# Narrowing 64-bit weights in an attention and MLP kernel: a parametric ReLU in place of a scaled copy and an and-or

## The chip, the cores and the metric

One core of a Trainium2 chip runs the whole program. It has TensorE for matrix products and transposes, VectorE and ScalarE for work along rows, GpSimd, SyncE that issues the transfers here, and 16 DMA engines. The metric is the device time of one execution in microseconds (us), lower is better.

## What is computed

The reference is an attention followed by two MLPs. The weights of both MLPs reach the kernel as 64-bit floats and are read as pairs of 32-bit words.

```python
# attention: q, k rotated; batch 4, 8 heads, 576 positions, 64 wide
scores = (1 / sqrt(64)) * (q_rot @ k_rot.T)
attn = exp(scores - max(scores)); attn = attn / (sum(attn) + 1e-09)
x = attn @ v                      # as 2304 tokens x 512
# first MLP: 512 -> 1536 -> 512
xn = x / sqrt(mean(x * x) + 1e-06) * rms_g
g = xn @ w_gate
x = (g * sigmoid(g) * (xn @ w_val)) @ w_out
# second MLP: 512 -> 1024 -> 1024 -> 512
h = ((x @ w1) * (x @ w2)) @ w3
out = h @ w_out
```

## The kernel before

Attention takes the heads in 16 pairs. A pair has nine tiles of 128 rows of scores. For each tile TensorE makes the scores (tile s), VectorE the row maximum (nm), ScalarE the Exp (p), TensorE the transposes (tp), ScalarE the high half and VectorE the low half of the transposed probabilities (pt), and TensorE the product with v (pv, two stages of it per pair). All matrix products are split into a high half, which is a cast to the fast float type, and a low half, which is what the cast left over; three products of halves (PASS) make one.

The first MLP works in six chunks of 384 tokens. Its input is scaled by the row norm (xr, function zz, line 684), transposed on TensorE (xp), and split (xc). For each of 12 slices of the hidden width TensorE makes gate and value (mm, line 308, 24 matmuls a slice), ScalarE the Silu (sg), VectorE the gated product u, ScalarE and VectorE the two halves of u (us), and TensorE the product with the output weights (acc, line 828, 12 matmuls a slice). The second MLP follows; most of its weights are narrowed while the first runs.

A weight is narrowed in steps. Its raw words (wraw, one buffer of 512 KB for 128x512 numbers) are loaded by SyncE. Step n0 is a scaled copy on ScalarE in place: the high word, read as a float, times 2^-111, which moves the exponent to that of a 32-bit float. Step n1 on VectorE shifts the low word right by 29 places; n2 shifts the high word left by 3 and puts the low word's bits in (the or, to tile wt). As the shift drops the sign, n3 takes the sign bit out of the high word and puts it into wt (the and-or). Then n4 on ScalarE casts the high half and n5 subtracts for the low half. These steps are a unit: 36 units for the first MLP, three for each of 12 slices (gate, value, output weights). For the second MLP function conv does the first four steps, 40 times, in jobs between the slices.

The order of work is fixed in two ways. Inside the attention it is written out by hand: ORDER gives the place of each step in a pair, ONCE that of each step of the first six units (W0.0 to W5.5, where W3.5 is step n3 of unit 5), and the first MLP's preparation. From unit 6 on, the units are written after the attention's program, and a scheduler places each instruction on its engine by its own estimate of when inputs and buffers are free. It can place them into the attention, as it does with the loads of units 6, 7 and 10 and the first steps of unit 10. Raw buffers come from a pool of three and, from the last pair on, from a second pool of two; a load must wait until the last reader of its buffer is done. PSUM tiles of transposes and matmuls come from one pool of four banks.

Of the kernel before, what the change touches and what calls it, by code (L numbers as in the profile page):

```python
# [8 lines left out]
F32 = mybir.dt.float32  # L9
F32R = mybir.dt.float32r  # L10
U32 = mybir.dt.uint32
I32 = mybir.dt.int32
AF = mybir.ActivationFunctionType
ALU = mybir.AluOpType
# [16 lines left out]

ONCE = {"WF.0": 0.058, "WF.1": 0.481, "W0.0": 2.871, "W1.0": 3.803, "W2.0": 4.815, "W0.1": 7.205, "W3.0": 7.711,
# [8 lines left out]
WARM = (22, 18, 3, 26)  # L41
NORM_AT = {5: (0, 1), 6: (1, 4), 7: (4, 6), 8: (6, 9), 9: (9, 12), 10: (12, 15), 11: (15, 18)}
# [21 lines left out]
def f(ap):  # L64
    return ap.bitcast(F32)
# [3 lines left out]
def kernel(  # L69
# [21 lines left out]
    nc = tc.nc  # L91
# [23 lines left out]
    def words(a):  # L115
        return a.bitcast(U32)
# [52 lines left out]
    wt_p = rpool("wt", WT)  # L169
# [37 lines left out]
    def rows(w, i, h=0):  # L207
        return words(w)[i * 128:(i + 1) * 128, h * 1024:(h + 1) * 1024]

    def unit(load, done):  # L210

        u = {}

        def raw():
            if not u:
                a = fifo.pop(0)
                u["lo"], u["hi"] = a[..., 0], a[..., 1]

        def n0():
            raw()
            nc.scalar.activation(out=f(u["hi"]), in_=f(u["hi"]), func=AF.Copy, scale=2.0**-111)

        def n1():
            raw()
            nc.vector.tensor_scalar(out=u["lo"], in0=u["lo"], scalar1=29, scalar2=None, op0=ALU.logical_shift_right)

        def n2():
            u["t"] = wt_p.tile([128, 512], F32, tag="t", name="wt")  # L230
            nc.vector.scalar_tensor_tensor(out=u["t"].bitcast(U32), in0=u["hi"], scalar=3, in1=u["lo"],
                                           op0=ALU.logical_shift_left, op1=ALU.bitwise_or)

        def n3():
            t = u["t"].bitcast(U32)
            nc.vector.scalar_tensor_tensor(out=t, in0=u["hi"], scalar=0x80000000, in1=t, op0=ALU.bitwise_and, op1=ALU.bitwise_or)

        return load, [n0, n1, n2, n3] + done(u)

    lo_eng = [nc.gpsimd]  # L240

# [9 lines left out]
    def unit_gv(kind, i, s):  # L251
        w = (w_gate, w_val)[s]

        def get():
            if s == 0:
                wgv[kind, i] = wtile([128, 2, 2, 512], "wgv", "wgv", i)
            return wgv[kind, i][:, 0, s], wgv[kind, i][:, 1, s]
        return unit(lambda: fetch(cols(w, i), 1), lambda u: split_steps(u, get))

    def unit_wo(kind, i):  # L260
        def get():
            t = wo[kind, i] = wtile([128, 2, 512], "wo", "wo", i)
            return t[:, 0], t[:, 1]
        return unit(lambda: fetch(rows(w_out, i)), lambda u: split_steps(u, get))
# [494 lines left out]
    def at(t, fn, *a):  # L759
        ev.setdefault(int(t // 1), []).append((t, len(ev.get(int(t // 1), ())), fn, a))  # L760
# [12 lines left out]
    once = {"NX": xload, "rst": rst, "nwt": nwt}  # L773
    for n_, t in ONCE.items():
        n_, u = n_.split(".") if "." in n_ else (n_, 0)
        u = int(u)
        if n_ == "WF":
            at(t, prefetch, u + 1)
        elif n_[0] == "W":
            at(t, units[u][1][int(n_[1])])  # L780
            if n_ == "W5":
                st[1] = max(st[1], u + 1)
        elif n_ in once:
            at(t, once[n_], 0)
        else:
            at(t, dict(sq=sq, z=zz, xp=xp, xh=xh, xl=xl)[n_[:-1]], 0, int(n_[-1]))
# [55 lines left out]
    def conv(src, c=None):  # L842

        u = {}

        def load():
            u["raw"] = raw = wst.tile([128, 512, 2], U32, tag="raw", name="wraw")
            if c is None:
                nc.sync.dma_start(out=raw.rearrange("p n t -> p (n t)"), in_=src)
            else:  # L850
                nc.sync.dma_start(out=raw.rearrange("p (c n) t -> p c (n t)", c=KC), in_=src.rearrange("(c p) n -> p c n", p=128))

        def rest():
            raw = u["raw"]
            lo, hi = raw[..., 0], raw[..., 1]
            nc.scalar.activation(out=f(hi), in_=f(hi), func=AF.Copy, scale=2.0**-111)
            nc.vector.tensor_scalar(out=lo, in0=lo, scalar1=29, scalar2=None, op0=ALU.logical_shift_right)
            t_ = wt_p.tile([128, 512], F32, tag="t", name="wt")
            t = t_.bitcast(U32)
            nc.vector.scalar_tensor_tensor(out=t, in0=hi, scalar=3, in1=lo, op0=ALU.logical_shift_left, op1=ALU.bitwise_or)  # L860
            nc.vector.scalar_tensor_tensor(out=t, in0=hi, scalar=0x80000000, in1=t, op0=ALU.bitwise_and, op1=ALU.bitwise_or)
            return t_
        return load, rest

    def tt(o, x, y, op=ALU.subtract):
# [156 lines left out]
    def gtile(shape, dt=F32):  # L1022
        return gv.tile(shape, dt, tag="g", name="gv")
# [82 lines left out]
    for k, batch in enumerate(todo):  # L1106
        run = []
        for g, s, P in batch:
            if (g, s) not in ws:
                ws[g, s] = weights(g, s)  # L1110
            t = gtile([128, 4, CH])
# [19 lines left out]
        n_ = (g + 1, s) if P == 2 else None  # L1131
# [60 lines left out]
    for i in range(NCH):  # L1192
# [9 lines left out]
        for o in range(NR):  # L1202
            t = gtile([128, DM])
# [62 lines left out]
```

## Time and profile before

| | |
|---|---|
| runs | 1107.41, 1105.12 and 1101.75 us, median 1105.12 |
| profiled execution | span 1101.9 us, granted TensorE clock 0.995 of full speed on average |
| busy share | TensorE 98%, VectorE 62%, ScalarE 51%, GpSimd 22% |
| attention | until about 309 us |
| first MLP | from there until about 770 us |

The span runs from the first to the last instruction of the one execution that was profiled. It is close to the fastest of the three runs and 3.2 us below their median. A row of the timeline below names the start, the duration, the engine, the line of the program, the operation, and what it writes and reads; in brackets stands the idle time of the engine just before it and what ended it.

### The profile page before, as it was taken

To read this page: it belongs to the slowest core of one execution; us is meant where nothing else is said; L and a number is where in the kernel's file an instruction comes from. 1 tells how busy PE (TensorE), PEld (TensorE's weight loads), DVE (VectorE), ACT (ScalarE), POOL (GpSimd) and SP (SyncE) were. 2 spreads that over 40 slices of the span, in tenths; PEclk is the share of its full clock that TensorE was granted. 3 is DMA by queue.
4 is the path that set the end of the run, shared out by engine and by line. 5 is a ranking of instruction groups with operands and counts; after the bars stand their busy time and mean duration, and the time that the engine had idled before them with its cause. 6 is when DMAs were issued, how large, how long until landed. Compare 5 with 4: busy or idle time off the path is not lost.

```text
span 1101.9 us, 18536 instructions
## 1 busy us (share of the span) xinstructions
PE 1077.5 (98%) x6669; PEld 1040.8 (94%) x6669; DVE 680.4 (62%) x1278; ACT 557.0 (51%) x1241; POOL 243.3 (22%) x359
## 2 busy tenths in 40 slices
PE   8899999999999999999999999999999999999998
PEld 7899999999889999999999999999999999888886
DVE  7899999999889953357555567552463443633220
ACT  5799998999865532233332333223353434422220
POOL 6878888799300000000000000000000000000000
PEclk9899999999999999999999999999999999999999
DMA  7677777776356531168492485635931415603441
GB/s 205 159 203 198 204 176 184 201 198 155 78 176 190 173 115 58 43 215 268 145 302 81 170 282 196 225 102 205 355 124 57 139 68 174 227 1 130 128 144 58
DMA packets 123547, 179.33 MB, mean 163 GB/s; under 512 B 18496, under 2 KB 85568, under 8 KB 123456
## 3 DMA queue, kind: packets, MB, share of 16 engines
q1 hardware_dynamic: 123456, 178.15, 53.6%
q8 instruction: 53, 0.87, 0.3%
q14 instruction: 38, 0.31, 0.1%
HBM read 99.53 MB, written 50.07 MB: 136 GB/s over the span
## 4 chain that ended last, share of the span: by engine, by line
PE 72%; DMA 11%; POOL 6%; DVE 5%; issue 2%; SPq 2%; ACT 1%; POOLq 0%; DVEq 0%; ACTq 0%
PE mm L308 22%; PE ps L1057 13%; PE acc L828 11%; PE ps L1200 9%; PE ps L1160 4%; PE s L496 4%; PE pv L569 3%; PE tp L513 3%; POOL rtmp L383 2%; DMA raw<-in_q_dram 2%; POOL rot L377 2%; DMA x2D<-x 1%; DMA vr<-in_v_dram 1%; DMA ks<-xy 1%; DMA xs<-xsD 1%
## 5 line engine op out<-in xcount | busy, mean ns | idle before, releaser
L308 PE MATMUL mm<-xc,wgv 128*128 128x384 f32 x1728 | 316.2, 335 | 0.2 <-ACT wgv L245 0.2
L308 PEld LDWEIGHTS mm<-xc,wgv 128*128 128x128 f32 x1728 | 299.9, 188 | 0.8 <-ACT wgv L245 0.7
L1057 PE MATMUL ps<-xs,cw 128*128 128x384 f32 x1008 | 176.3, 335 | 1.2 <-DMA xs<-xsD 1.2
L1057 PEld LDWEIGHTS ps<-xs,cw 128*128 128x128 f32 x1008 | 174.6, 188 | 2.1 <-DMA xs<-xsD 1.9
L828 PE MATMUL acc<-us,wo 128*128 128x384 f32 x864 | 166.2, 335 | 2.4 <-ACT us L107 2.2
L828 PEld LDWEIGHTS acc<-us,wo 128*128 128x128 f32 x864 | 150.7, 188 | 4.2 <-ACT us L107 3.2
L496 PE MATMUL s<-ks,qs 128*128 128x288 f32 x640 | 122.3, 318 | 8.6 <-DMA ks<-xy 5.0
L501 DVE TENSOR_REDUCE nm<-s 128x1 f32<-128x576 f32 x144 | 107.8, 750 | 14.2 <-PE s L496 12.5
L507 ACT ACTIVATE p<-s,nm 128x576 f32<-128x576 f32 x144 | 107.5, 746 | 10.8 <-DVE nm L501 10.2
L496 PEld LDWEIGHTS s<-ks,qs 128*128 128x128 f32 x640 | 91.8, 193 | 11.5 <-issue 5.5
L1200 PE MATMUL ps<-wp,us 128*128 128x512 f32 x432 | 98.1, 389 | 0.0
L1200 PEld LDWEIGHTS ps<-wp,us 128*128 128x128 f32 x432 | 81.1, 188 | 16.8
L107 ACT CAST us<-u 128x384 fp32r<-128x384 f32 x72 | 36.8, 511 | 119.0 <-DVE u L320 115.0
L521 DVE TENSOR_TENSOR pt<-tp,pt 128x512 fp32r<-128x512 f32 x144 | 94.5, 681 | 1.3 <-ACT pt L517 0.6
L320 DVE SCALAR_TENSOR_TENSOR u<-mm,sg 128x384 f32<-128x384 f32 x72 | 39.8, 553 | 86.1 <-PE mm L308 80.9
L517 ACT CAST pt<-tp 128x512 fp32r<-128x512 f32 x144 | 82.5, 585 | 2.9 <-PE tp L513 2.0
L513 PE MATMUL tp<-idn,p 128*128 128x128 f32 x576 | 83.5, 277 | 0.5 <-DVE x L609 0.2
L569 PE MATMUL pv<-pt,vs 128*128 128x288 f32 x512 | 81.0, 300 | 2.6 <-DVE pt L521 2.5
L569 PEld LDWEIGHTS pv<-pt,vs 128*128 128x128 f32 x512 | 70.8, 188 | 3.1 <-DVE pt L521 3.1
L513 PEld LDWEIGHTS tp<-idn,p 128*128 128x128 f32 x576 | 68.7, 143 | 2.1 <-PE s L496 0.6
L318 ACT ACTIVATE sg<-mm 128x384 f32<-128x384 f32 x72 | 35.1, 488 | 66.1 <-PE mm L308 65.8
L108 DVE TENSOR_TENSOR us<-u,us 128x384 fp32r<-128x384 f32 x72 | 40.0, 556 | 36.3 <-ACT us L107 36.2
(138 smaller groups left out, 1357.0 us busy)
## 6 DMA issues: line engine op xcount, KB each, us to landing
ks<-xy SPq DMA_DIRECT2D x62, 288.0 KB, 5.0
wraw<-in_moe_w_dram SPq DMA_DIRECT2D x32, 512.0 KB, 5.4
xsD<-xo SPq DMA_DIRECT2D x28, 384.0 KB, 3.9
xs<-xsD SPq DMA_DIRECT2D x14, 768.0 KB, 8.2
wraw<-in_moe_w_out_dram SPq DMA_DIRECT2D x20, 512.0 KB, 4.6
qs<-xy SPq DMA_DIRECT2D x62, 160.0 KB, 2.8
uD<-gv SPq DMA_DIRECT2D x12, 768.0 KB, 3.6
us<-uD SPq DMA_DIRECT2D x24, 384.0 KB, 3.9
```

The lines of the kernel that those rows point to most:

```text
L308: nc.tensor.matmul(ps[:, 0:CH], lhsT=w[:, a, s, c * 128:(c + 1) * 128], rhs=x[:, b_, c, :], start=(i == 0), stop=(i == 3 * KC - 1))
L496: nc.tensor.matmul(ps[:, hf, 0:HS], lhsT=l, rhs=r_[:, hf * HS:(hf + 1) * HS], start=(i == 0), stop=(i == n - 1))
L501: nc.vector.tensor_reduce(out=nm, in_=s_ps[p, t][:, :, 0:HS], axis=AX.XY, op=ALU.max, negate=True)
L507: nc.scalar.activation(out=pp.rearrange("p (a b) -> p a b", a=2), in_=s_ps.pop((p, t))[:, :, 0:HS], func=AF.Exp, bias=s_max.pop((p, t)), s ...
L513: nc.tensor.transpose(ps[:, c, :], p_sb[p, t][:, LF + c * 128:LF + (c + 1) * 128], idn)
L517: lastins["act"] = nc.scalar.copy(out=hi, in_=src)
L521: lastins["dve"] = nc.vector.tensor_tensor(out=lo, in0=src, in1=f(hi), op=ALU.subtract)
L569: nc.tensor.matmul(ps[:, 0:HS], lhsT=l.rearrange("p s d -> p (s d)"), rhs=r, start=(i == 0), stop=(i == 8))
L828: nc.tensor.matmul(acc[o][:, 0:CH], lhsT=wo[kind, n][:, a, o * 128:(o + 1) * 128], rhs=us[:, b_], start=(n == first and s == 0), stop=(n = ...
L1057: nc.tensor.matmul(b[ch], lhsT=w[i][:, p_, c * 128:(c + 1) * 128], rhs=x[i][:, r, c], start=(first and ch != 1 and n == 0), stop=(n == 5), ...
L1160: nc.tensor.matmul(p_, lhsT=t[a][:, c], rhs=woc[c][:, b_], start=(i == 0), stop=(i == 3 * NJ - 1))
L1200: nc.tensor.matmul(ac[o], lhsT=us[j // 2][:, a, j % 2, o * 128:(o + 1) * 128], rhs=wp[j][:, b_], start=(j == 0 and s == 0), stop=(j == NJ ...
```

## The change

Step n0 becomes a Prelu: for a positive number the result is the number times 2^-111, as before; for a negative one it is multiplied by 2^32 as well. The larger exponent of the negative numbers sets the bit that n2's shift by 3 moves to the place of the sign. Step n3 is left out, in the units and in conv; in ONCE, n3's entries go, and the two steps behind it are renumbered at the times they had.

```diff
-    "W3.2": 49.378, "sq2": 56.9, "W0.4": 60.614, "W1.3": 61.7, "W5.1": 63.645, "W4.2": 66.556, "W2.3": 69.949,
...
+    "sq2": 56.9, "W0.4": 60.614, "W1.3": 61.7, "W4.1": 63.645, "W3.2": 66.556, "W2.3": 69.949,
...
+    def narrow(hi):
+
+        nc.scalar.activation(out=f(hi), in_=f(hi), func=AF.Prelu, scale=2.0**-111, alpha=2.0**32)
...
         def n0():
             raw()
-            nc.scalar.activation(out=f(u["hi"]), in_=f(u["hi"]), func=AF.Copy, scale=2.0**-111)
+            narrow(u["hi"])
...
-        def n3():
-            t = u["t"].bitcast(U32)
-            nc.vector.scalar_tensor_tensor(out=t, in0=u["hi"], scalar=0x80000000, in1=t, op0=ALU.bitwise_and, op1=ALU.bitwise_or)
-
-        return load, [n0, n1, n2, n3] + done(u)
+        return load, [n0, n1, n2] + done(u)
...
-            if n_ == "W5":
+            if n_ == "W4":
...
         def rest():
             raw = u["raw"]
             lo, hi = raw[..., 0], raw[..., 1]
-            nc.scalar.activation(out=f(hi), in_=f(hi), func=AF.Copy, scale=2.0**-111)
+            narrow(hi)
             nc.vector.tensor_scalar(out=lo, in0=lo, scalar1=29, scalar2=None, op0=ALU.logical_shift_right)
-            t_ = wt_p.tile([128, 512], F32, tag="t", name="wt")
-            t = t_.bitcast(U32)
-            nc.vector.scalar_tensor_tensor(out=t, in0=hi, scalar=3, in1=lo, op0=ALU.logical_shift_left, op1=ALU.bitwise_or)
-            nc.vector.scalar_tensor_tensor(out=t, in0=hi, scalar=0x80000000, in1=t, op0=ALU.bitwise_and, op1=ALU.bitwise_or)
-            return t_
+            t = wt_p.tile([128, 512], F32, tag="t", name="wt")
+            nc.vector.scalar_tensor_tensor(out=words(t), in0=hi, scalar=3, in1=lo, op0=ALU.logical_shift_left, op1=ALU.bitwise_or)
+            return t
```

The scheduler's order moves in more places than the diff names. The first is VectorE's order at the start of the first MLP, behind the second slice's u. Before, these rows stand there (wraw is a shift, wt<-wraw the or, wt<-wraw,wt the and-or, xr the scaling of the second chunk's input, xc its low half):

```order
L320 SCALAR_TENSOR_TENSOR u<-mm,sg 128x384
L675 TENSOR_TENSOR rstd<-rstd,nt 128x3
L231 SCALAR_TENSOR_TENSOR wt<-wraw 128x512
L684 SCALAR_TENSOR_TENSOR xr<-xr,rstd,g 128x512 x3
L227 TENSOR_SCALAR wraw<-wraw 128x512
L108 TENSOR_TENSOR us<-u,us 128x384
L236 SCALAR_TENSOR_TENSOR wt<-wraw,wt 128x512
L699 TENSOR_TENSOR xc<-xp,xc 128x4x128
```

After, an or of unit 8 stands directly ahead of that u, a shift and a norm step directly behind it, and then these rows (line numbers are those of the changed program):

```order
L246 TENSOR_TENSOR wo<-wt,wo 128x512
L671 TENSOR_TENSOR nt<-nt,ms 128x3
L233 SCALAR_TENSOR_TENSOR wt<-wraw 128x512 x3
L106 TENSOR_TENSOR us<-u,us 128x384
L672 TENSOR_TENSOR nt<-cst,nt 128x3
L229 TENSOR_SCALAR wraw<-wraw 128x512
L246 TENSOR_TENSOR wgv<-wt,wgv 128x512 x2
L673 TENSOR_TENSOR rstd<-rstd,nt 128x3
L246 TENSOR_TENSOR wo<-wt,wo 128x512
L229 TENSOR_SCALAR wraw<-wraw 128x512
L233 SCALAR_TENSOR_TENSOR wt<-wraw 128x512 x2
L682 SCALAR_TENSOR_TENSOR xr<-xr,rstd,g 128x512 x3
```

The scaling of xr, which came third behind that u, has moved behind three shifts, four low halves, five ors and us.

The second place is TensorE's order at the same time, from the first matmul of the first MLP. Before:

```order
L308 MATMUL mm<-xc,wgv 128x384 x48
L828 MATMUL acc<-us,wo 128x384 x14
L692 MATMUL xp<-idn,xr 128x128 x4
L308 MATMUL mm<-xc,wgv 128x384 x24
L692 MATMUL xp<-idn,xr 128x128 x4
L828 MATMUL acc<-us,wo 128x384 x10
L692 MATMUL xp<-idn,xr 128x128 x4
```

After:

```order
L306 MATMUL mm<-xc,wgv 128x384 x48
L826 MATMUL acc<-us,wo 128x384 x24
L690 MATMUL xp<-idn,xr 128x128 x4
L306 MATMUL mm<-xc,wgv 128x384 x24
L690 MATMUL xp<-idn,xr 128x128 x8
L306 MATMUL mm<-xc,wgv 128x384 x24
```

All 24 output matmuls of the first two slices now stand ahead of the first transposes of the second chunk's input.

The third place is ScalarE's order in the attention around the narrowing of unit 10. Before, it stands in the last pair (lt is the last tile's part of pt):

```order
L547 CAST lt<-lp 64x512
L507 ACTIVATE p,sums<-s,nm 128x576
L517 CAST pt<-tp 128x4x128
L507 ACTIVATE p,sums<-s,nm 128x576
L517 CAST pt<-tp 128x4x128
L223 ACTIVATE wraw<-wraw 128x512
L517 CAST pt<-tp 128x4x128
```

After, one pair earlier:

```order
L545 CAST lt<-lp 64x512
L505 ACTIVATE p,sums<-s,nm 128x576
L210 ACTIVATE wraw<-wraw 128x512
L515 CAST pt<-tp 128x4x128
L505 ACTIVATE p,sums<-s,nm 128x576
L515 CAST pt<-tp 128x4x128 x2
```

The narrowing now stands ahead of the first cast of its pair instead of the third. Its shift on VectorE and its load on SyncE have moved one pair earlier as well; the load stands right behind that pair's loads of v (vr), as it stood behind the last pair's before. ScalarE's order still has two table loads, at the start and ahead of the first Silu.

## Rows read from the trace of the kernel before

**Rows 1.** Page, part 1: busy us, share of the span, instructions

```profile
PE 1077.5 (98%) x6669; PEld 1040.8 (94%) x6669; DVE 680.4 (62%) x1278; ACT 557.0 (51%) x1241; POOL 243.3 (22%) x359
```

**Rows 2.** Windows of 20 us: length, busy (count) by engine, clock, DMA share, GB/s

```profile
360.00:380.00 20.00, 20.00 (x117) 20.00 (x117) 18.70 (x36) 11.39 (x21) 0.00 (x0) 1.00 0.50 158
...
640.00:660.00 20.00, 20.00 (x117) 20.00 (x116) 12.75 (x25) 8.02 (x16) 0.00 (x0) 1.00 0.87 294
```

**Rows 3.** Groups of VectorE: the and-or; count, busy us, mean ns, idle before

```profile
L861 DVE SCALAR_TENSOR_TENSOR wt<-wraw,wt 128x512 uint32<-128x512 uint32 x40 | 26.7, 686 | 0.4
...
L236 DVE SCALAR_TENSOR_TENSOR wt<-wraw,wt 128x512 uint32<-128x512 uint32 x36 | 25.9, 732 | 0.0
```

**Rows 4.** Groups of ScalarE, columns as in rows 3

```profile
L507 ACT ACTIVATE p<-s,nm 128x576 f32<-128x576 f32 x144 | 107.5, 746 | 10.8 <-DVE nm L501 10.2 <-ACT pt L517 0.2
L517 ACT CAST pt<-tp 128x512 fp32r<-128x512 f32 x144 | 82.5, 585 | 2.9 <-PE tp L513 2.0
...
L223 ACT ACTIVATE wraw<-wraw 128x512 f32<-128x512 f32 x36 | 24.7, 688 | 27.1 <-DMA wraw<-in_moe_w_gate_dram 11.2 <-DMA wraw<-in_moe_w_out_dram 8.2 <-DMA wraw<-in_moe_w_val_dram 7.5
...
L318 ACT ACT_TABLE_LOAD x1 | 1.3, 1283 | 0.0
```

**Rows 5.** Timeline of VectorE and TensorE at two and-ors of the attention

```profile
117.94 0.90 DVE L236 SCALAR_TENSOR_TENSOR wt<-wraw,wt 128x512 uint32<-128x512 uint32 x1
...
121.57 0.77 PE L496 MATMUL s<-ks,qs 128*128 128x288 f32 x4 [0.48 <-ACT p L507]
...
171.80 1.55 DVE L236 SCALAR_TENSOR_TENSOR wt<-wraw,wt 128x512 uint32<-128x512 uint32 x1
...
174.75 0.63 PE L583 MATMUL op<-idn,osb 128*128 128x128 f32 x4 [0.36 <-DVE pt L521]
```

**Rows 6.** Timelines of three engines around the load of unit 10

```profile
278.62 0.68 DVE L236 SCALAR_TENSOR_TENSOR wt<-wraw,wt 128x512 uint32<-128x512 uint32 x1
...
280.34 0.54 SPq L201 DMA_DIRECT2D wraw<-in_moe_w_val_dram  x1
...
284.69 1.15 DVE L227 TENSOR_SCALAR wraw<-wraw 128x512 uint32<-128x512 uint32 x1 [2.10 <-DMA wraw<-in_moe_w_val_dram]
...
286.50 1.34 PE L569 MATMUL pv<-pt,vs 128*128 128x288 f32 x8 [2.55 <-DVE pt L521]
```

**Rows 7.** Windows: length, TensorE's busy time (count), granted clock, DMA share, GB/s

```profile
288.00:291.50 3.50, 3.50 (x17) 0.51 0.00 0
672.00:676.00 4.00, 3.35 (x19) 1.00 0.91 310
```

**Rows 8.** Timelines of three engines one pair earlier

```profile
258.18 0.68 DVE L231 SCALAR_TENSOR_TENSOR wt<-wraw 128x512 uint32<-128x512 uint32 x1
...
262.31 0.61 SPq L348 DMA_DIRECT2D vr<-in_v_dram  x1
...
266.68 1.23 PE L569 MATMUL pv<-pt,vs 128*128 128x288 f32 x8
```

**Rows 9.** Timeline of TensorE at the start of the first MLP

```profile
320.99 0.66 PE L692 MATMUL xp<-idn,xr 128*128 128x128 f32 x4 [0.17 <-DVE xr L684]
...
326.02 1.99 PE L828 MATMUL acc<-us,wo 128*128 128x384 f32 x10
```

**Rows 10.** Timeline of VectorE in the same stretch

```profile
318.63 0.43 DVE L227 TENSOR_SCALAR wraw<-wraw 128x512 uint32<-128x512 uint32 x1 [1.00 <-DMA wraw<-in_moe_w_out_dram]
...
319.58 0.68 DVE L231 SCALAR_TENSOR_TENSOR wt<-wraw 128x512 uint32<-128x512 uint32 x1
320.19 2.07 DVE L684 SCALAR_TENSOR_TENSOR xr<-xr,rstd,g 128x512 f32<-128x512 f32 x3
...
322.51 0.55 DVE L108 TENSOR_TENSOR us<-u,us 128x384 fp32r<-128x384 f32 x1
...
324.18 1.28 DVE L231 SCALAR_TENSOR_TENSOR wt<-wraw 128x512 uint32<-128x512 uint32 x2
325.38 0.68 DVE L248 TENSOR_TENSOR wo<-wt,wo 128x512 fp32r<-128x512 f32 x1
```

**Rows 11.** Timeline of TensorE near the end of the first MLP

```profile
672.65 2.62 PE L828 MATMUL acc<-us,wo 128*128 128x384 f32 x12 [1.50 <-ACT us L107]
```

More of the change, by code (lines that the diff above doesn't have):

```diff
@@ L30 @@
     "RR": 16.466, "lv": 16.571, "OLR": 16.975, "OA1": 16.977, "OR1": 17.165, "X": 17.215, "XD": 17.967}
-ONCE = {"WF.0": 0.058, "WF.1": 0.481, "W0.0": 2.871, "W1.0": 3.803, "W2.0": 4.815, "W0.1": 7.205, "W3.0": 7.711,
[7 rows of a table removed]
+ONCE = {"WF.0": 0.058, "WF.1": 0.481, "W0.0": 2.871, "W1.0": 3.803, "W2.0": 4.815, "W0.1": 7.205,     "W1.1": 8.606, "WF.2": 16.22, "W2.1": 16.41, "W0.2": 19.818, "WF.3": 26.556, "W3.0": 30.057,
[5 rows of a table added]
     "xl0": 139.778, "xp2": 140.495, "xh2": 141.275, "xl2": 141.913}
```

10 rows, old and new, of the table ONCE are left out of this document.

## The prediction

> **What bounds the kernel now.** I read the page's busy times first: TensorE works 98% of the span, VectorE 62%, ScalarE 51% [rows 1]. So a saving on VectorE only counts where TensorE stands still for VectorE, and the second reading looked for such a place. At 360 to 380 us VectorE is busiest, 18.70 of 20 us, and TensorE still shows 117 matmuls and no idle time [rows 2]; that is 20/117 = 0.171 us a matmul, the pace it also has at 640 to 660 us, where VectorE is busy 12.75 us. A VectorE at 94% therefore does not slow TensorE. What is left to win or lose are single waits, and the order of the instructions decides them: each engine runs its own in the order written, so one that waits holds everything behind it.
>
> **What is removed, in bulk.** The and-or is 36 instructions of 25.9 us in the units and 40 of 26.7 us in the second layer's weights [rows 3]: 52.6 us of VectorE's time. TensorE covers it nearly everywhere. If the cover were gone (VectorE alone as the bound) it would be worth up to the 52.6 us; it isn't gone in any stretch longer than a few us, so I cost the bulk at 0 and go through the single places.
>
> **What the Prelu costs.** No Prelu is in the trace. The scaled copy that it replaces takes 688 ns; on the same engine a cast of the same size (128x512) takes 585 ns and an Exp over 576 columns 746 ns [rows 4]. So one instruction changes by between -0.10 and +0.06 us; I take 0, since the copy itself is an ACTIVATE with a scale and the Prelu has the same operands and one more constant. In the stretches above ScalarE is busy 11.39 of 20 us [rows 2], which hides either end: 21 instructions per 20 us at 0.06 would be 1.3 us of 8.6 idle.
>
> A load of the activation table takes 1283 ns, and the kernel has one at the first Silu [rows 4]. If Prelu were not in the same table as Exp, each of the seven narrowings that the order has inside the attention would put two of these between two Exps: 7 x 2 x 1.283 = 18 us of ScalarE in a stage in which it is nearly full, and 69 more afterwards. The Trainium skill, "ScalarE activation tables: per-element evaluation and per-set limits", section "What a function is on this engine", says that functions in different sets are one table load of 1283 ns apart and those of one set need none; by that rule the sum would be +18 us or 0, according to the set. The changed program's ScalarE still has two loads in all, at the same two places, so this stays a small rival.
>
> **Attention: the and-ors that TensorE waited for.** Six and-ors stand in the attention. I looked at TensorE's idle time behind each and found it after two: the one at 117.94 us takes 0.90 us, the row maximum behind it is late, the Exp behind that too, and TensorE idles 0.48 us at 121.57; the one at 171.80 takes 1.55 us and TensorE idles 0.36 at 174.75 [rows 5]. Without them both waits go: 0.84 us, and somewhat more because the matmuls just ahead were already issued at less than pace. I take **-1.1 us**; bounds 0 (another instruction is as late) and -2.0.
>
> **Attention: the late weight load moves one pair earlier.** The longest wait of the attention's end belongs to the weights of unit 10. The and-or of unit 5 (278.62 us) was the last reader of a raw buffer; the load into it was issued at 280.34 and landed 4.3 us later; VectorE's shift waited 2.10 us for it and took 1.15, and ScalarE's narrowing stood ahead of attention work in the same way; the PV matmuls started at 286.50 after 2.55 us of idle time, 1.9 us behind the landing [rows 6]. Behind it the granted clock was 0.51 for 3.5 us [rows 7], the lower of TensorE's two levels (1.2 of 2.4 GHz): 1.7 us more lost. Together about 4.3 us.
> After the change the buffer is free once unit 5's or is done, at 258.18 + 0.68 us [rows 8], a pair earlier. But the load also stands one pair earlier on SyncE, right behind the value load that was issued at 262.31 and took 0.61 [rows 8]: it goes out at about 262.9 and, at the 4.3 us it took before, lands at 267.2. Its narrowing stands one pair earlier too: on ScalarE ahead of the casts of that pair's transposed probabilities, on VectorE ahead of the subtractions that follow. With the same 1.9 us from landing to PV, the PV matmuls that ran at 266.68 [rows 8] start at 269.1, 2.4 us late. So the same wait comes a pair sooner, with the same fall of the clock behind it. I take **0**, bounds -1.5 and +1.5.
>
> **Start of the first MLP.** Here the scheduler's order changes most, and this term carries the forecast. In the trace TensorE goes from the first 48 gate and value matmuls to 14 output matmuls, then to the transposes of the next chunk's input (320.99 us, hardly a wait), 24 matmuls of that chunk, and only then to the other ten output matmuls, 1.99 us from 326.02 [rows 9]. The transposes need xr scaled by VectorE, which runs at 320.19 us, straight behind the first or of unit 8 [rows 10].
> In the new order VectorE does a great deal ahead of that scaling. Follow it from the landing of unit 8's weights, at 318.63 us [rows 10], with durations from rows 4 and 10: narrowing on ScalarE 0.69, the or 0.64 (two take 1.28), u 0.55 (as the low half of us, an operation of the same size): 320.5. Then a shift 0.43, a low half 0.68 (the ScalarE cast it subtracts is done by then), three ors 1.92, the low half of us 0.55: 324.1. Then a shift 0.43, three low halves 2.04, another shift 0.43, two ors 1.28: 328.3. The first scaling takes 0.69 (2.07/3): done at 329.0. Neighbouring instructions overlap by some hundredths, which makes it less, and four small norm steps stand between, which make it more; I take 328.65 for the start of the transposes, with 328.0 and 329.4 as ends.
> So the transposes start 328.65 - 320.99 = 7.7 us later. TensorE's new order uses part of that: all 24 output matmuls come first, so ten of them, 1.7 us at 0.171, are behind it. The lag is 7.7 - 1.7 = **+6.0 us**, ends 5.3 and 6.7. TensorE idles in three pieces (for the cast of us, for its low half, for the scaling). Afterwards the trace shows TensorE at its pace [rows 2], so nothing gives the lag back.
>
> **The clock behind that wait.** Behind the 2.55 us wait the granted clock fell to 0.51; behind an idle time of 1.50 at 672.65 it stayed at 1.00 [rows 7, 11]. The new pieces are 2 to 3 us each, but with work between them, so the fall is possible and not certain: 0 to 1.7 us (the price found above). I take **+0.5**.
>
> **The end of the first MLP.** At 672.65 us TensorE waits 1.50 us for ScalarE's cast of us, which waits for VectorE's u, late behind two ors, two and-ors and a norm chain [rows 11]. The two and-ors (2 x 0.68) go, and the new order of TensorE has 24 matmuls of the next chunk between the output matmuls. I take **-1.0**, bounds -2 and +1 (a new order here could lose as well).
>
> **Sum.** -1.1 + 0 + 6.0 + 0.5 - 1.0 = +4.4 us on the profiled execution's span of 1101.9 us [rows 1]: 1106.3. That execution lies 3.2 us under the median of the three runs, 1105.12; the same 4.4 us on the median gives **1109.5 us**. The runs spread over 0.5%, about 5.5 us, which is about what a measurement of this kernel can tell from no change.
>
> **The rivals.**
> *The removal is hidden and the order costs nothing.* The transposes do not wait because VectorE is far enough ahead (the loads land sooner, since buffers come free sooner). Then only -1.1 and -1.0 count, less some 0.6 for places where a new order may lose: about -1.5 us, 1103.6. For it: VectorE has less to do. Against it: the new order puts thirteen instructions of 0.4 to 0.7 us ahead of the scaling, and the landing that starts them does not come sooner. It decides if the scaling ends before 322.7 us (320.99 and the 1.7 us of work that has moved ahead). Chance 0.20.
> *Faster.* The load of unit 10 lands in time. Its buffer is free 20 us earlier, so if the load goes 2.4 us sooner than I think, the whole 4.3 us of wait and clock go, and with the -1.1 and -1.0, and half the lag at the start of the MLP, the time is -6.4 + 3 = -3.4, or without any lag -6.4: 1098.7 to 1101.7. It decides at SyncE: the load must land 1.9 us before 266.68, so go out by 260.5. Against it the value load that stands ahead of it at 262.31 [rows 8]. Chance 0.13.
> *Clearly slower.* The lag of 6.7, the clock down for the next chunk (1.7), unit 10's wait 1.5 longer, no gain at 672: +9 to +10, 1114 to 1115. Chance 0.12.
> *Table loads.* +18 us or more, above 1120; chance 0.02. That the Prelu does not place the sign is possible as well and would not change the time: the Trainium skill, "ScalarE: Activation LUTs", section "Step-by-step: what each stage is for", says that the per-side slope is not reachable from a kernel, and that every function has the same throughput. No row here shows either.
> *My forecast*, +2 to +8: chance 0.53, 1107 to 1113.
>
> **How the numbers follow.** Cases of both signs hold much of the chance. The range 1101.5 to 1114 takes in the hidden case and the slower one's start, and leaves out the faster one's larger half (0.07), the far end of the clearly slower one (0.08) and the table loads (0.02). Faster by over 0.5% (under 1099.6) is the faster rival's lower half and some of the hidden one with scatter: 0.11. Slower by over 0.5% (over 1110.6) is 0.22 of my forecast's 0.53 (its upper part: 4.4 us is not far under the bound of 5.5) and both slower rivals' 0.14: 0.36. The rest, 0.53, is within 0.5%.
>
> **What would show it.** The page: VectorE near 628 us busy, TensorE still 97 to 98%, ScalarE as before. In detail: no idle behind 117.94 and 171.80; a wait of about 2.5 us on PV matmuls near 266 to 269 instead of 286; at 319 to 329 us three TensorE waits, the last for the scaling of xr, 5 to 7 us in all; the matmul pace at 340 to 400 unchanged. The forecast is wrong if the transposes of the second chunk start before 323 us, if the PV wait is gone, or if a Prelu takes over 0.8 us.

## The result and the profile after

The changed kernel takes 1111.47 us in the median of four runs (1109.54 to 1112.61), the kernel before 1103.43 in the median of four, one more than the table above has. The recorded ratio is 1.0081, with a 95% interval from 1.0062 to 1.0099; the two medians alone make 1.0073. The profiled execution's span is 1107.8 us, 5.9 more than before. That execution is the fastest of the four. The forecast was 1109.5, with 1101.5 to 1114 as range.

The first part of the page after, with busy us, share of the span and instructions of each engine:

```profile
PE 1075.6 (97%) x6669; PEld 1039.5 (94%) x6669; DVE 634.2 (57%) x1202; ACT 556.9 (50%) x1241; POOL 238.9 (22%) x359
```

Beside [rows 1], VectorE has 76 instructions less and is 46.2 us less busy (the 52.6 us of [rows 3] count each alone; neighbours overlap). TensorE does the same 6669 instructions in a longer span. So the engine that was relieved is not the one that sets the time, as forecast, and the question is where TensorE stands.

Two marks cut the span in three, the first matmul of the first MLP (mm) and the first of the second MLP's product (ps). TensorE's timeline of the kernel before at both:

```profile
308.81 0.43 PE L308 MATMUL mm<-xc,wgv 128*128 128x384 f32 x1
...
770.08 5.23 PE L1057 MATMUL ps<-xs,cw 128*128 128x384 f32 x28
```

And TensorE's timeline after, the marks and the waits between and behind them:

```profile
269.08 0.80 PE L494 MATMUL s<-ks,qs 128*128 128x288 f32 x4 [3.35 <-ACT p L505]
...
307.56 8.57 PE L306 MATMUL mm<-xc,wgv 128*128 128x384 f32 x48
...
319.41 0.62 PE L826 MATMUL acc<-us,wo 128*128 128x384 f32 x2 [1.19 <-ACT us L105]
321.67 3.28 PE L826 MATMUL acc<-us,wo 128*128 128x384 f32 x10 [1.64 <-DVE us L106]
326.91 0.66 PE L690 MATMUL xp<-idn,xr 128*128 128x128 f32 x4 [1.97 <-DVE xr L682]
...
335.19 2.36 PE L306 MATMUL mm<-xc,wgv 128*128 128x384 f32 x12 [0.49 <-DVE u L318]
...
364.90 0.61 PE L826 MATMUL acc<-us,wo 128*128 128x384 f32 x2 [0.38 <-ACT us L105]
...
376.92 0.62 PE L826 MATMUL acc<-us,wo 128*128 128x384 f32 x2 [1.15 <-ACT us L105]
...
773.55 1.73 PE L1053 MATMUL ps<-xs,cw 128*128 128x384 f32 x8
...
807.83 7.38 PE L1053 MATMUL ps<-xs,cw 128*128 128x384 f32 x41 [2.65 <-DVE xs L106]
```

The attention ends 308.81 - 307.56 = 1.25 us earlier. From mark to mark the first MLP takes 465.99 us instead of 461.27, 4.7 more. From the second mark to the end of the span it is 334.25 instead of 331.8, 2.4 more. The sum is the 5.9. Inside the first MLP, the three waits at 319 to 327 us are the forecast ones, the two at 365 and 377 are new, and the 1.50 us wait of [rows 11] is gone.

VectorE's timeline after, from the or ahead of the second slice's u to the scaling of xr:

```profile
317.03 0.69 DVE L233 SCALAR_TENSOR_TENSOR wt<-wraw 128x512 uint32<-128x512 uint32 x1
...
317.71 0.55 DVE L318 SCALAR_TENSOR_TENSOR u<-mm,sg 128x384 f32<-128x384 f32 x1
318.18 0.42 DVE L229 TENSOR_SCALAR wraw<-wraw 128x512 uint32<-128x512 uint32 x1
...
318.58 0.68 DVE L246 TENSOR_TENSOR wo<-wt,wo 128x512 fp32r<-128x512 f32 x1
...
319.25 1.89 DVE L233 SCALAR_TENSOR_TENSOR wt<-wraw 128x512 uint32<-128x512 uint32 x3
321.06 0.55 DVE L106 TENSOR_TENSOR us<-u,us 128x384 fp32r<-128x384 f32 x1
...
321.99 0.43 DVE L229 TENSOR_SCALAR wraw<-wraw 128x512 uint32<-128x512 uint32 x1 [0.31 <-DMA wraw<-in_moe_w_val_dram]
322.33 0.68 DVE L246 TENSOR_TENSOR wgv<-wt,wgv 128x512 fp32r<-128x512 f32 x1
323.29 0.69 DVE L246 TENSOR_TENSOR wgv<-wt,wgv 128x512 fp32r<-128x512 f32 x1 [0.27 <-ACT wgv L243]
...
323.97 0.69 DVE L246 TENSOR_TENSOR wo<-wt,wo 128x512 fp32r<-128x512 f32 x1
324.57 0.42 DVE L229 TENSOR_SCALAR wraw<-wraw 128x512 uint32<-128x512 uint32 x1
324.91 1.28 DVE L233 SCALAR_TENSOR_TENSOR wt<-wraw 128x512 uint32<-128x512 uint32 x2
326.11 2.07 DVE L682 SCALAR_TENSOR_TENSOR xr<-xr,rstd,g 128x512 f32<-128x512 f32 x3
```

VectorE is hardly ever idle here. It is busy with weights that are needed later, and TensorE waits for the two results, us and xr, that stand behind them (for the first wait, at 319.41 us, u itself stood behind an or). In [rows 10] the scaling began 0.61 us behind the or at 319.58.

### The profile page after: what moved, and what is told of

It reads as the page before. It is cut to its first block, busy times and chain, and to the rows that moved or that the text cites. A ratio compares the mean times of both kernels' runs of the same rounds, so it can differ in the third digit from the quotient of the medians.

```text
span 1107.8 us, 18457 instructions
## 1 busy us (share of the span) xinstructions
PE 1075.6 (97%) x6669; PEld 1039.5 (94%) x6669; DVE 634.2 (57%) x1202; ACT 556.9 (50%) x1241; POOL 238.9 (22%) x359
## 4 chain that ended last, share of the span: by engine, by line
PE 84%; DMA 8%; DVE 5%; ACT 1%; SPq 1%; issue 1%; POOL 0%; POOLq 0%; ACTq 0%; DVEq 0%
PE mm L306 23%; PE ps L1053 13%; PE acc L826 12%; PE ps L1196 9%; PE s L494 7%; PE pv L567 6%; PE tp L511 5%; PE ps L1156 3%; PE lp L541 1%; PE qtp L428 1%; PE op L581 1%; DMA wraw<-in_moe_w_val_dram 1%; DMA wraw<-in_moe_w_out_dram 1%; DMA ks<-xy 1%; DMA wraw<-in_moe_w_gate_dram 1%
## 5 line engine op out<-in xcount | busy, mean ns | idle before, releaser
L210 ACT ACTIVATE wraw<-wraw 128x512 f32<-128x512 f32 x76 | 51.0, 684 | 32.1 <-DMA wraw<-in_moe_w_val_dram 10.6
```

What stands on the lines that cost most here:

```text
L210: nc.scalar.activation(out=f(hi), in_=f(hi), func=AF.Prelu, scale=2.0**-111, alpha=2.0**32)
```

## The experiments

Each ratio is to the kernel before on the same chip, with its 95% interval. Theory A: the order costs the time. Theory B: the Prelu does. Theory C: the loss comes from the second layer's conversions. Theory D: the weights land too late for TensorE, and the order only names the wait.

**The two halves of the edit, apart.** The first kernel has the Prelu and keeps the and-or, the second has the old copy and no and-or, so its weights lose their sign. Their orders are row for row those of the kernel before and of the changed one.

```diff
 e1, on the kernel before, in n0 and in conv
-func=AF.Copy, scale=2.0**-111
+func=AF.Prelu, scale=2.0**-111, alpha=2.0**32
 e2, on the changed kernel
-func=AF.Prelu, scale=2.0**-111, alpha=2.0**32
+func=AF.Copy, scale=2.0**-111
```

> The Prelu alone: the scaled copy becomes the Prelu, and VectorE's and-or stays (it puts the same sign in again). Every engine's order is row for row that of the kernel before. Theory A (the order costs the time, the Prelu nothing): ratio to before 1.000, within 0.002, the same waits as before (2.5 us for the late load at about 286 us, transposes at 321 us), Prelu within 0.02 us of the copy's 0.688. Theory B (the Prelu costs the time, by its own duration or by what it does to its readers): ratio 1.006 to 1.010.

> The order alone: the scaled copy stays, the and-or goes, so the weights lose their sign and the result is another one. Every engine's order is row for row that of the changed kernel. Theory A: ratio 1.006 to 1.010, with the changed kernel's waits (three at 319 to 327 us, 2.65 at 808, none of 1.5 at 672). Theory B: 0.998 to 1.000, as only work was taken away.

Measured: e1 1.0015 (0.9998 to 1.0032), 1102.32 us; e2 1.0115 (1.0093 to 1.0137), 1113.64 us. E1 came as theory A has it, e2 above its range of 1.006 to 1.010. The slowdown goes with the missing and-or and its order, not with the Prelu. (No run leaves the and-or out and keeps the old order; that the order costs the time, and not the missing work as such, is read from the waits and from the runs below.) In e1's groups of ScalarE the narrowing of the 36 units is, beside 688 ns in [rows 4]:

```profile
L223 ACT ACTIVATE wraw<-wraw 128x512 f32<-128x512 f32 x36 | 24.7, 690 | 27.1 <-DMA wraw<-in_moe_w_gate_dram 11.9 <-DMA wraw<-in_moe_w_out_dram 8.0 <-DMA wraw<-in_moe_w_val_dram 7.3
```

Theory B falls. That e2 is above the changed kernel's own 1.0081, with intervals that overlap, has a place in part: the same wait in the attention (3.86 us at 269.08) had the clock fall behind it there, so that the next four score matmuls took 1.22 us instead of 0.80. Of the 3.5 us between the two profiled executions, 1.5 are made in the attention and 1.9 behind the second mark, where the order is the same.

**The two sets of weights, apart.** In e3 conv keeps the and-or, in e4 the units keep it.

```diff
 e3, on the changed kernel, in conv behind the or
+            nc.vector.scalar_tensor_tensor(out=words(t), in0=hi, scalar=0x80000000, in1=words(t), op0=ALU.bitwise_and, op1=ALU.bitwise_or)
 e4, on kernel e1, in conv
-            nc.vector.scalar_tensor_tensor(out=t, in0=hi, scalar=0x80000000, in1=t, op0=ALU.bitwise_and, op1=ALU.bitwise_or)
```

> The change in the 36 units of the first MLP alone; the 40 conversions of the second layer's weights have the Prelu and keep the and-or. Theory A (the loss is at the start of the first MLP): attention -0.5, late load -1.5, start of the MLP +5.5, the waits at 360 to 380 us +2.1, sum +5.6 us, ratio 1.005 (1.003 to 1.007). Theory C (the loss comes from the second layer's conversions and the product stage): ratio under 1.002.

> The other half: the and-or is left out in the 40 conversions of the second layer's weights alone. Theory A: order and time up to 460 us as before (transposes at 321 us); the 1.5 us wait at 672 us goes (-2), a wait in the product stage may come (+2): ratio 0.998 to 1.002. Theory C: 1.005 or more.

Measured: e3 1.0112 (1.0087 to 1.0138), e4 0.9998 (0.9979 to 1.0017). All of the loss comes with the 36 units; theory C falls. E3 lost more than I expected, as the wait for xr was 3.46 us instead of 1.97, the 3.80 us wait in the attention had the clock fall behind it, and the wait in the product stage, which my sum left out, came although conv kept its and-or.

**Moving the order on the changed kernel.** Four edits that change nothing but the order, on more than one engine each: e5 writes the first transposes of the second chunk behind the matmuls of the first chunk's third slice; e6 keeps unit work of slices 0 to 2 behind us of its slice; e7 keeps unit 10's narrowing behind the attention; e8 is e6 and e7 together.

```diff
 e5
-NORM1 = ((0, 4), (4, 9), (9, 12), (12, 18))
+NORM1 = ((0, 4), (4, 9), (9, 9), (9, 18))
 e6, ahead of finish
+                for ins in gate_ins if si < 3 else ():
+                    after.enter_context(tc.issue_after(ins.ins))
 e7
-                if si == 0:
+                if si < 3:
                     for ins in lastins.values():
```

> The changed kernel with one number of NORM1 changed: the first transposes of the second chunk's input are written behind the matmuls of the first chunk's third slice instead of ahead of them. Theory A (TensorE stands behind the transposes while matmuls of the first chunk are ready, since VectorE does ors and low halves first): the 2 us wait for xr goes, TensorE has matmuls to do while us is late too, and the loss at 300 to 340 us falls from 8.4 us (13 on the chip of the last runs) to 1 to 3; ratio to the kernel before 1.000 to 1.005. Theory D (the weights' loads land too late for the matmuls, so that the order only names another wait): the wait moves to the matmuls of the third slice, ratio stays 1.008 to 1.012.

> The changed kernel, where the narrowing of units that is written after slices 0 to 2 is kept behind us of the same slice on each engine. The order then has us and the scaling of xr ahead of most ors and low halves. Theory A: the three waits at 319 to 327 us shrink to under 1.5 us in all, ratio 0.998 to 1.004, and as the narrowing of unit 10 leaves the attention with it, 3 to 6 us more go: 0.995 to 1.000. Theory D: matmuls wait for wgv instead, 4 us or more, ratio 1.006 or more.

> The changed kernel with the narrowing of units up to 11 kept behind the attention's last steps (before: up to 7). Only unit 10 moves. Theory A: the wait of 3 us for its load at 266 us goes with the clock's fall behind it, the start of the MLP stays as in the changed kernel: 3 to 6 us less than that, ratio 1.002 to 1.007. Rival: the narrowing is missing at the start of the MLP, where ScalarE and VectorE are behind as it is, and the lag there grows by 1 to 2 us: ratio 1.006 to 1.010.

> The two holds of the last two runs together. Theory A: no wait for a weight's load in the attention and none over 1 us at the start of the MLP: 5 to 8 us below the kernel before (its own late load cost 4.3), ratio 0.993 to 0.998. Theory D: 1.004 or more.

Measured: e5 1.0018 (1.0000 to 1.0036), e6 1.0039 (1.0023 to 1.0054), e7 1.0042 (1.0026 to 1.0058), e8 1.0031 (1.0018 to 1.0044). E5 and e7 came as theory A has them; e6 and e8 missed its ranges for them, 0.995 to 1.000 and 0.993 to 0.998. The order of e8 is row for row that of e6 on every engine, so e8 repeats e6 and is not a further edit. TensorE's timelines of e5 and then of e6:

```profile
327.58 1.01 PE L826 MATMUL acc<-us,wo 128*128 128x384 f32 x2 [2.71 <-ACT us L105]
```

```profile
316.06 2.03 PE L826 MATMUL acc<-us,wo 128*128 128x384 f32 x10 [0.58 <-DVE us L106]
321.37 0.66 PE L690 MATMUL xp<-idn,xr 128*128 128x128 f32 x4 [3.28 <-DVE xr L682]
```

In e5 the wait for xr is gone and one for us is left, in the third slice. From mark to mark it takes 462.03 us, 4.0 less than the changed kernel; another 2.6 go behind the second mark, in the product stage below. In e6 the waits for us are 0.58, but the one for xr has grown to 3.28: VectorE still had two ors, a shift that waited 0.66 for its load and a low half that waited 0.78 for ScalarE ahead of the scaling. So theory D has a small part in it. No run of the four waits for wgv there, which D wanted. The hold did shorten the first MLP: from mark to mark e6 and e8 take 462.3 and 461.9 us, against 466.0. But behind the second mark they take 339.2 and 336.2 instead of 334.3, which theory A had not looked at, and e6 also has unit 10 out of the attention, so that as a whole it gains nothing clear over e7.

**The product stage.** The timelines of SyncE, VectorE and ScalarE show where 2.5 us are lost near 804 us in some kernels. Before, and then after (sb are the sums' inputs, st a sum, gv a step of the products, uD a result that is stored):

```profile
786.81 0.32 SPq L916 DMA_DIRECT2D sb<-x2D  x1
788.05 0.37 SPq L1128 DMA_DIRECT2D uD<-gv  x1
789.68 0.32 SPq L916 DMA_DIRECT2D sb<-x2D  x1
...
799.20 0.56 DVE L866 TENSOR_TENSOR st<-sb 128x384 f32<-128x384 f32 x1 [1.30 <-DMA sb<-x2D]
```

```profile
791.35 0.37 SPq L1124 DMA_DIRECT2D uD<-gv  x1
792.72 2.90 SPq L912 DMA_DIRECT2D sb<-x2D  x2
...
804.17 0.51 ACT L105 CAST xs<-sb 128x384 fp32r<-128x384 f32 x1 [0.95 <-DMA sb<-x2D]
...
805.48 1.36 DVE L1123 SCALAR_TENSOR_TENSOR gv<-gv 128x1152 f32<-128x1152 f32 x1
806.76 0.55 DVE L862 TENSOR_TENSOR st<-sb 128x384 f32<-128x384 f32 x1
```

The third load of sb stands ahead of the store before and behind it after, so it goes out with the fourth, 19.2 us behind the mark at 773.55 instead of 16.7 behind that at 770.08. It lands 1.5 us later behind the mark (at 804.17, where before VectorE has it at 799.20), but VectorE begins the sum 4.1 us later. The rest is VectorE's own order: three steps of the products, the last at 805.48, have moved ahead of the sum. TensorE waits 2.65 us for xs. The traces of e1, e4, e5 and e9 to e12 have the load ahead of the store, the sum ahead of those three steps, and no wait for VectorE's xs there; e2, e3, e6, e7 and e8 have both the other way and wait 1.7 to 2.9 us. That was read from the fourteen traces and not tried by moving the load or the sum alone.

**Combined, and with the and-or back.** e9 is e5 and e7, e10 is e5, e6 and e7, both on the changed kernel. e11 has e7's edit and e12 all three on the kernel before.

> The changed kernel with the later transposes (run e5) and with unit 10 after the attention (run e7). Theory A: e5's loss of 6 us at 260 to 280 us goes, the third load for the second MLP's sums stays ahead of the store of uD on SyncE, so no 2.5 us wait near 804 us; what is left is the wait for us at about 323 us with the clock behind it (4 to 6 us). Ratio to the kernel before 0.994 to 0.999. Rival (gains do not add up, as unit 10's narrowing lengthens the wait for us): 1.000 to 1.003.

> The changed kernel with later transposes, unit 10 after the attention, and the weights' narrowing behind us in slices 0 to 2. Theory A: no wait over 1 us between 260 and 400 us, none of 2.5 us near 804 us (the third load is ahead of the store of uD): 5 to 8 us below the kernel before, ratio 0.993 to 0.996. Rival: some new wait takes half of it, 0.997 to 1.000.

> The kernel before (scaled copy and and-or) with unit 10 after the attention. Theory A: its 4.3 us of wait and clock at 286 us go; the order at the start of the MLP becomes like the changed kernel's (24 output matmuls ahead of the transposes, but the scaling of xr stays behind us and one and-or only), so 1 to 3 us come back there: ratio 0.996 to 1.000. If the order at the start costs nothing with the and-or: 0.995.

> The same three changes of order as run e10, on the kernel before, with scaled copy and and-or: what is the and-or worth when neither kernel has those waits? Theory A (VectorE's and-ors are hidden behind TensorE): within 0.002 of run e10, so 0.993 to 0.998. Rival (the and-or costs time at the start of the MLP or at 672 us): 2 to 4 us above run e10.

Measured: e9 0.9994 (0.9979 to 1.0008), e10 0.9984 (0.9970 to 0.9998), e11 0.9957 (0.9943 to 0.9972), e12 1.0021 (1.0006 to 1.0036). E11, at 1096.86 us, is the fastest and beats both kernels. It lies between the two cases expected for it, as e9 does; e10 came in its rival's range and missed theory A's. In e9 and e10 the weights' work makes new waits at the start of the first MLP. ScalarE's timeline of e9:

```profile
322.22 0.68 ACT L210 ACTIVATE wraw<-wraw 128x512 f32<-128x512 f32 x1 [0.16 <-DMA wraw<-in_moe_w_out_dram]
323.63 0.66 ACT L210 ACTIVATE wraw<-wraw 128x512 f32<-128x512 f32 x1 [0.72 <-DMA wraw<-in_moe_w_gate_dram]
...
324.71 0.51 ACT L105 CAST us<-u 128x384 fp32r<-128x384 f32 x1
```

VectorE does low halves and an or ahead of u, which begins only at 323.71, and the cast of us stands behind narrowings that wait for loads; TensorE waits 3.70 us for it at 325.27. E10 has none of these, and instead waits of 1.72 and 0.95 us for u and sg at 338 and 347. TensorE's timeline of e11 shows how little the same place can cost:

```profile
314.82 0.61 PE L828 MATMUL acc<-us,wo 128*128 128x384 f32 x2 [0.30 <-ACT us L107]
315.82 2.03 PE L828 MATMUL acc<-us,wo 128*128 128x384 f32 x10 [0.39 <-DVE us L108]
317.69 0.60 PE L692 MATMUL xp<-idn,xr 128*128 128x128 f32 x4
```

And VectorE's in e11:

```profile
315.22 0.55 DVE L108 TENSOR_TENSOR us<-u,us 128x384 fp32r<-128x384 f32 x1
315.68 0.68 DVE L236 SCALAR_TENSOR_TENSOR wt<-wraw,wt 128x512 uint32<-128x512 uint32 x1
316.29 2.07 DVE L684 SCALAR_TENSOR_TENSOR xr<-xr,rstd,g 128x512 f32<-128x512 f32 x3
```

TensorE's order is the new one here as well (24 output matmuls ahead of the transposes). But us and the scaling come early on VectorE, and 0.7 us are lost where the changed kernel loses 4.8. So TensorE's own order does not cost this by itself; it costs it where VectorE's and ScalarE's order makes us and xr late. (It has a part: e5, which lets TensorE do matmuls first, lost less.) E11 beside e7 is the change once more without unit 10's wait: 0.9957 against 1.0042, again about 0.8% slower without the and-or. E12 beside e10 turns it round: with all three edits the and-or costs 1103.48 - 1100.14 = 3.3 us between the medians, the rival's size (2 to 4). The two profiled executions differ by 1.3 us only; in e12's first MLP, 2.0 us longer there, the largest wait is one of 2.02 us at 331.07 for wgv, whose or and and-or come late. The sign of the change's worth thus depends on which order the scheduler makes of it.

## Why the prediction was right, step by step

**The bulk at nothing**: right. VectorE is relieved by 46 us and no stretch of TensorE's pace became faster.

**The Prelu at nothing**: right, 690 ns against 688, and e1 bounds it at -0.02% to +0.32% of the time. ScalarE has two table loads of 1283 ns after as before, so the sum is the one with 0, and the rival with table loads fell. By the Trainium skill's rule on sets ("ScalarE activation tables: per-element evaluation and per-set limits", "What a function is on this engine") Prelu shares a set with Exp and one with Silu. The Prelu does place the sign: e5 to e10, with it and without the and-or, give the reference's output, and e2, without either, does not. The page that the prediction names for the other case (the Trainium skill, "ScalarE: Activation LUTs", "Step-by-step: what each stage is for") has the slope out of a kernel's reach; these runs show it within reach.

**The attention's and-ors at -1.1 us**: of the right size, not told apart by a run of its own. The wait at 174.75 is gone; in e1, which has the and-ors, it is there with 0.40. The wait at 121.57 became one of 0.28 for ks, but in e1 it is 0.84 and for ks as well, so it was not the and-or's alone. The attention as a whole ends 1.25 us earlier, although its first pair lost 1.1 us more to the load of ks (5.92 us against 4.81; over the fourteen traces it is 4.23 to 6.21), where the change has no part that I can name. With the 0.9 us of the next point, some 1.4 us are left for the and-ors and for scatter.

**Unit 10's load at 0**: the landing was right to a tenth of a microsecond, what followed it only in part. SyncE's and VectorE's timelines after:

```profile
262.92 0.54 SPq L199 DMA_DIRECT2D wraw<-in_moe_w_val_dram  x1
...
267.15 0.71 DVE L229 TENSOR_SCALAR wraw<-wraw 128x512 uint32<-128x512 uint32 x1 [2.20 <-DMA wraw<-in_moe_w_val_dram]
```

The load goes out at 262.9 and lands at 267.1 as forecast. TensorE idles 3.35 us instead of my 2.4 (it was the score matmuls ahead of PV that waited, for an Exp behind the narrowing), and the clock, which I had falling, stayed in this execution: 3.35 against 4.3, -0.9, inside the bounds. In e2, e3 and e5, which have the same wait, it fell. E11, which has no such wait, is 0.43% under the kernel before (4.5 us between the medians), though its order differs in other places too.

**The start of the first MLP at +6.0, and the clock at +0.5**: right. TensorE idles 1.19 + 1.64 + 1.97 + 0.49 = 5.3 us at 319 to 335; before, the waits of that stretch are 0.72, 0.17 and 0.19. The ten output matmuls at 321.67 took 3.28 us, 1.3 more than those of [rows 9]; the granted clock after was

```profile
320.00:330.00 10.00, 6.39 (x30) 0.83 0.87 286
```

So 4.2 of idle time and 1.3 of clock, 5.5 of the 6.5 forecast. The transposes start 326.91 - 307.56 = 19.4 us behind the first matmul instead of 12.2: 7.2 later, where I had 7.7. The landing that starts VectorE's work came 8.7 us behind the first matmul instead of 9.8, against what the prediction said of it, but short waits of 0.31 and 0.27 us on the way, which it had not counted, took back part of that. Another statement was wrong without a number hanging on it: the 24 matmuls behind the first transposes belong to the first chunk's third slice, not to the second chunk. TensorE had ready work and stood ahead of it, which e5 used.

**The end of the first MLP at -1.0**: the wait of 1.50 went whole. It also went in e4, so it belongs to the second layer's and-ors. But its size was that of one execution: in e1, e3, e11 and e12, which keep them, it is 0.41 to 0.65, so the 1.50 is more than the wait mostly costs.

**What the sum did not have**: two waits of 0.38 and 1.15 us at 365 and 377, and 2.4 us in the product stage. At 364.90 and 376.92 it is the mechanism of the MLP's start once more. ScalarE's timeline after:

```profile
363.76 0.70 ACT L210 ACTIVATE wraw<-wraw 128x512 f32<-128x512 f32 x1 [1.68 <-DMA wraw<-in_moe_w_gate_dram]
364.36 0.49 ACT L105 CAST us<-u 128x384 fp32r<-128x384 f32 x1
```

A narrowing that waits 1.68 us for its load stands ahead of the cast of us. I had looked for losses in the stretches where the trace of before had waits, and the new order made some where it had none. With these the profiled execution is +5.9 instead of +4.4. (The pieces named for the first MLP, 5.5 + 1.5 - 1.5, make 0.8 more than the 4.7 from mark to mark; that rest I have not placed.) The rival in which the removal is hidden and the order costs nothing fell: its bound for the end of the first scaling was 322.7 us, and it began at 326.11. The medians differ by 8.0 us, 2.1 more than the profiled executions. The profiled one had a mean granted clock of 0.995; the two slowest of the four had 0.990 and 0.989, and where they lost it no trace shows. So the largest term and its mechanism were right, but that the time came within 2.0 us of 1109.5 is in part luck: the change was 8.0 us and not 4.4, and the sum started from 1105.12, where the median with the fourth run is 1103.43.

## What to carry to other kernels

Work taken from an engine off the bound is worth what TensorE waits for it, here at most about 3 us in two or three waits; the new order that a scheduler makes of the shorter program can cost more than that, so compare the orders engine by engine before you count the saving. Look for work for later (here weights) that stands ahead of something TensorE needs now, above all where it waits for a load. When such an edit comes out slower, separate instruction and order with two kernels, one with the new instruction in the old order (e1) and one with the old instruction in the new order (e2). Then read every stage to its end: beside the changed kernel, e6 won 3.7 us in the first MLP, where it was meant to, and lost 5.0 behind the second mark, where I had not looked.

## What was not expected of the hardware

The clock's fall does not follow from the length of the wait just ahead of it. Behind 2.55 us it fell to 0.51 [rows 6, 7]; behind the changed kernel's 3.35 us it did not:

```profile
269.00:275.00 6.00, 5.92 (x48) 1.00 0.06 15
```

Behind 3.86, 3.80 and 3.66 us at the same place in e2, e3 and e5 it fell again (granted clock 0.77, 0.63 and 0.50 over 266 to 272 us), and behind e6's 3.28 us at 321.37 it did not (1.00 over 320 to 330 us). What decides it was not tried.
